# Two buffers for one tile's exponentials, a freer ScalarE order in the third tile, and a higher planner priority for four steps

## The chip, the cores and the metric

The kernel runs on one core of one Trainium2 chip. The metric is the device time of one execution in microseconds (us); of several executions the median counts. A step of the kernel is worth what it adds to the time at which the last output lands.

## The reference

The input is queries, keys and values for 4 batches, 8 heads, 576 positions and 64 dimensions a head, and the weights of two layers.

```python
scores = q @ k.T / sqrt(64)                 # heads 0-3: a local mask, 32 back; heads 4-7: a strided mask, every 32nd
attn = softmax(where(mask, scores, -1e9)) @ v
x = attn, heads side by side                # 2304 tokens x 512
h = maximum(x @ w_in1, 0)                   # first layer, 2048 wide
y = (h * h) @ w_out1
u = y @ w_in2                               # second layer
g = maximum(u, 0) + alpha * minimum(u, 0)
out = g @ w_out2
```

## The kernel before

**Tiles.** Tokens are cut into seven tiles for the first layer (`TILES`): tiles 0, 1 and 2 have 256 columns each, tiles 3 to 6 have 384. The second layer has six tiles of 384. Each tile goes through 16 slices `f` of the 2048-wide layer. One slice of one tile is a *step* `n`: steps 0 to 31 are tiles 0 and 1, interleaved by `FIRST`; steps 32 to 47 are tile 2, the third tile; then come tiles 3 to 6 and, from step 112 on, the second layer.

**One step.** Every float is carried as a high and a low part, so a product is three matmuls. `emit_h` puts 12 matmuls into the one PSUM bank `h` (line 566). `emit_g` reads that bank on ScalarE (Relu, line 578), squares it into the high part `gh` (line 579) and once more in place (line 580). `emit_gl` takes the difference on VectorE as the low part `gl` (line 594). `emit_y` adds 8 matmuls with `gh` and 4 with `gl` into the output banks (line 620). Since `h` is one bank, the matmuls of the next step's `h` wait until line 578 has read it. The second layer has lines 583 to 588 in the place of 578 to 580.

**Attention.** It is computed piece by piece while earlier tiles run. A `Unit` is local attention for some blocks: `scores` (line 245, or 249 for tiles 0 and 1), `softmax_a` on VectorE (mask and scale into the tile `e`, line 259; maximum, line 263), `softmax_b` on ScalarE (exponential with row sum, line 267), `softmax_c` (reciprocal on VectorE, lines 274 and 275; then scaling, on VectorE line 277 for tiles 0 to 2 and on ScalarE line 282 for later ones), `turn` (transposes of `e`, line 289), `turn_copy` (line 293), `values` (line 299), `emit_hi` and `emit_lo` (lines 308 and 315, the tile's `x`). `e` has one buffer, so line 259 of a unit waits for line 289 of the unit before. `Dense` is the same for the strided heads of tiles 0 and 1 (lines 340 to 400). `Strided` is strided attention of later tiles, nearly all on VectorE (lines 450, 457, 491, 498). The four units of tile 3 and its strided work are put into the iterations of the third tile (units at iterations 32, 34, 37 and 40).

**Weights.** Each of the 16 weight slots of the first layer is loaded once and converted by `convert_a` to `convert_d` on ScalarE and VectorE (lines 159 to 191), beside the steps of tiles 0 and 1. Line 191 is the last operation of a slot.

**What sets the order.** The program emits instructions in the order of `run`. SyncE issues in emission order throughout. TensorE, VectorE and GpSimd run in an order that a planner fixes when the kernel is compiled: at each point of its modelled time it gives an engine the instruction that is ready and was emitted earliest. ScalarE is under the planner up to iteration 31 and in emission order from iteration 32 on (the two `manual_schedule` regions at the end). On the chip each engine then runs its list in that order, and an instruction at its head that waits holds all behind it.

Of the kernel before, what the change touches and what calls it, by code (L numbers as in the profile page):

```python
# [16 lines left out]
P = 128  # L17
# [53 lines left out]
def attn_moe_moe2(  # L71
# [39 lines left out]
    NF = w_in1.shape[0]  # L111
# [17 lines left out]
    def psum(tag):  # L129
        return ppool.tile([P, 512], F32, tag=tag, name=f"ps_{tag}")  # L130
# [12 lines left out]
    def load_w(layer, f):  # L143

        t = wpool.tile([P, 2, 512, 2], U32, tag=f"w{f}", name="wraw")
        for h in range(2):
            src = W[layer][h][f].bitcast(U32).rearrange("p (f t) -> p f t", t=2)
            nc.sync.dma_start(out=t[:, h], in_=src)
        raws[layer, f] = t
# [48 lines left out]
    def x_tile(t):  # L198
        if t not in x_sb:
            kw = {"bufs": 1} if t == 2 else {}  # L200
            x_sb[t] = tuple(
                xpool.tile([P, NC, COLS[t]], F32R, tag=nm[:2] if t != 2 else nm, name=f"{nm}{t}", **kw)
                for nm in ("xh_c", "xl_c")
            )
        return x_sb[t]


    class Unit:


        bufs = None
# [40 lines left out]

        def softmax_a(self):
            n = self.n
            self.e = self.new("e", [P, 3, 96], bufs=1)[:, 0:n]
            self.st = apool.tile([P, 3, 4], F32, tag="st", name="stat", bufs=4)[:, :, 0:n]
            s = self.s[:, 0:96 * n].rearrange("p (n c) -> p n c", c=96)
            m = mfirst if self.first else mloc
            nc.vector.scalar_tensor_tensor(
                out=self.e, in0=s, scalar=SCALE,  # L260
                in1=m.unsqueeze(1).to_broadcast([P, n, 96]), op0=ALU.mult, op1=ALU.add,
            )
            nc.vector.tensor_reduce(out=self.st[:, 0, :], in_=self.e, op=ALU.max, axis=AX.X, negate=True)
# [284 lines left out]
    steps = [(0, t, f) for t, f in FIRST]  # L548
# [6 lines left out]
    def cols_of(n):  # L555
        return COLS[steps[n][1]] if n < SECOND else T

    def emit_h(n):
        l, t, f = steps[n]
        xh, xl = x_tile(t) if l == 0 else x2[t]  # L560
        w = wslot[l, f]
        h = psum("h")
        for c in range(NC):
            whi, wlo = w[:, 0, c * P:(c + 1) * P], w[:, 1, c * P:(c + 1) * P]
            for i, (a, b) in enumerate(((whi, xh), (whi, xl), (wlo, xh))):
                nc.tensor.matmul(  # L566
                    h[:, 0:b.shape[2]], a, b[:, c, :], start=(c == 0 and i == 0), stop=(c == NC - 1 and i == 2)
                )
        hs[n] = h

    def emit_g(n):
        l, t, f = steps[n]
        m = cols_of(n)
        h = hs.pop(n)[:, 0:m]
        g = gpool.tile([P, T], F32, tag="g", name="g")[:, 0:m]
        gh = gpool.tile([P, T], F32R, tag="gh", name="gh")[:, 0:m]
        if l == 0:
            nc.scalar.activation(out=g, in_=h, func=AF.Relu)  # L578
            nc.scalar.activation(out=gh, in_=g, func=AF.Square)  # L579
            nc.scalar.activation(out=g, in_=g, func=AF.Square)  # L580
        else:
            u = spool.tile([P, T], F32, tag="pr", name="u", bufs=2)
            nc.scalar.activation(out=g, in_=h, func=AF.Relu)  # L583
            nc.scalar.activation(out=u, in_=h, func=AF.Relu, scale=-1.0)  # L584
            nc.vector.scalar_tensor_tensor(  # L585
                out=g, in0=u, scalar=nalpha[:, f:f + 1], in1=g, op0=ALU.mult, op1=ALU.add
            )
            nc.scalar.activation(out=gh, in_=g, func=AF.Copy)  # L588
        g_sb[n] = (g, gh)

    def emit_gl(n):
        g, gh = g_sb[n]
        gl = gpool.tile([P, T], F32R, tag="gl", name="gl")[:, 0:cols_of(n)]
        nc.vector.tensor_tensor(  # L594
            out=gl, in0=g, in1=gh.bitcast(F32), op=ALU.subtract
        )
        g_sb[n] = (gh, gl)
# [70 lines left out]
    def at(when, n, fn, *args):  # L668
        when.setdefault(n, []).append((fn, args))

    def emit(when, n):
        for fn, args in when.get(n, []):
            fn(*args)
# [79 lines left out]
    def run(ns):  # L753
        for n in ns:
            l, t, f = steps[n]
            emit(starts, n)
            emit(loads, n)
            emit_gl(n)
            emit(front, n)
            if n + 1 < len(steps):  # L760
                emit_h(n + 1)
            emit(fill, n)
            emit(tensor_part, n)
            if n + 1 < len(steps):
                emit_g(n + 1)
            emit(tail_part, n)
            emit_y(n)
            if f == NF - 1:
                evac(t, l)

    outs = {}
    with tc.manual_schedule(engines={mybir.EngineType.SP}):
        def part(tag, *sizes):

            whole = wpool.tile([P, sum(sizes)], F32, tag=tag, name=f"att_{tag}")
            return [whole[:, sum(sizes[:i]):sum(sizes[:i + 1])] for i in range(len(sizes))]

        masks, de11 = part("w11", 224, 512)
        mfirst, mstr = masks[:, 0:96], masks[:, 96:224]
        bufs = {}  # L780
        for t, tags in enumerate((("w7", "w8", "w9", "w10"), ("w15", "w14", "w13", "w12"))):
            n = D * (t + 1)
            a = part(tags[0], 640, 640, 384, 384)
            v = part(tags[1], *(512,) * 4)
            pt = part(tags[2], *(512,) * 4)
            d = part(tags[3], *((512, 512, 256, 256) if t == 0 else (768, 768, 512)))
            for p in range(2):
                bufs[t, "L", p] = {
                    "qk": a[p].rearrange("p (n c) -> p n c", c=D + 96), "v": v[p][0:96].rearrange("p (n c) -> p n c", c=P),
                    "e": a[2 + p].rearrange("p (n c) -> p n c", c=96), "pt": pt[p][0:96],  # L790
                }
                bufs[t, "D", p] = {
                    "qk": d[p], "v": v[2 + p][0:n].rearrange("p (n c) -> p n c", c=P),
                    "e": d[2 + p] if t == 0 or p == 0 else de11, "pt": pt[2 + p][0:n],
                }
        units = []
        for t, kind in ORDER:
            p = sum(isinstance(x, Unit if kind == "L" else Dense) and x.t == t for x in units)
            if kind == "L":
                units.append(Unit(t, p, 0))  # L800
                units[-1].bufs = bufs[t, "L", p]
            else:
                units.append(Dense(t, p, bufs[t, "D", p]))

        def load_consts():
            nc.sync.dma_start(out=ident, in_=consts[:, 0:128])
            nc.sync.dma_start(out=mloc, in_=consts[:, 128:224])
            nc.sync.dma_start(out=masks, in_=consts[:, 224:448])

        for i, x in enumerate(units):  # L810
            x.load_qk()
            if i == 0:
                load_consts()
            if i > 0:
                units[i - 1].load_v()
            for f, w in enumerate(LOAD_AFTER):
                if w == i:
                    load_w(0, f)
        units[-1].load_v()
        for f, w in enumerate(LOAD_AFTER):  # L820
            if w >= len(units):
                load_w(0, f)
        plan()

        todo = []
        for i, unit in enumerate(units):
            for j, (name, tick) in enumerate(STAGES):
                banks = BANKS.get(name)
                args = (banks[i % len(banks)],) if banks else ()
                todo.append((i + tick + (BACK if unit.t else 0), 1, i, j, getattr(unit, name), args))  # L830
        for f, ticks in enumerate(EARLY):
            for j, (fn, tick) in enumerate(zip((convert_a, convert_b, convert_c, convert_d), ticks)):
                todo.append((tick, 0, f, j, fn, (0, f)))
        for tick, *_, fn, args in sorted(todo, key=lambda x: x[:4]):
            n = sum(tick >= x for x in TICKS)
            if n:
                at(starts, n - 1, fn, *args)
            else:
                fn(*args)
        emit_h(0)  # L840
        emit_g(0)
        run(range(2 * NF))
    with tc.manual_schedule(engines={mybir.EngineType.SP, mybir.EngineType.Activation}):
        run(range(2 * NF, len(steps)))


_OUTS = [((2304, 512), "float32")]
# [104 lines left out]
```

## Time and profile before

| | us |
|---|---|
| three runs | 894.0, 895.06, 895.51 |
| median | 895.06 |
| the profiled execution, its own time | 895.83 |
| its span in the trace | 894.0 |
| TensorE busy in the span | 870.4 |
| VectorE busy | 553.5 |
| ScalarE busy | 455.1 |

The profile's page says which engine is busy when; the windows cut the span into stretches; the waits say who waited for whom; the timelines list one engine's instructions in order, with the idle time before each and what ended it in brackets. [...] The profiled execution took 0.77 us more than the median of the runs and 1.83 us more than its span.

### The profile page before, as it was taken

The numbers are of one execution on the slowest core, as the hardware profiler recorded it, in microseconds if no ns is written. First come the engines' busy times: TensorE is split into PE (matmuls) and PEld (weight loads), VectorE is DVE, ScalarE is ACT, GpSimd is POOL, SyncE is SP. The second block draws the span as 40 slices with busy tenths as digits, with TensorE's granted clock in tenths as the row PEclk, the third lists the DMA queues.
The fourth block names the chain that finished last, engine by engine and source line by source line (L and its number), as shares of the span: only waits on it lengthen the run. The fifth ranks groups of instructions, "written<-read, shape, count | busy, mean of one in ns | idle before, by whom it ended". The sixth has DMA issues, their size and how long they took to land.

```text
span 894.0 us, 13787 instructions
## 1 busy us (share of the span) xinstructions
PE 870.4 (97%) x5448; PEld 817.4 (91%) x5448; DVE 553.5 (62%) x877; ACT 455.1 (51%) x1063; POOL 1.5 (0%) x10
## 2 busy tenths in 40 slices
PE   6799999899999999999999999999999999999997
PEld 5699989799999999999999999999999999999996
DVE  5999999949678796794598983233233333333322
ACT  6889655455545554545577664334334334334332
POOL 0000000000000000000000000000000000000000
PEclk9999999999999999999999999999999999999999
DMA  9990402111212212100687200100100100100000
GB/s 295 393 339 2 153 8 86 45 52 62 71 51 73 68 56 73 49 8 26 241 271 267 82 10 27 36 9 29 34 10 30 33 10 30 33 9 32 5 1 36
DMA packets 33537, 70.34 MB, mean 79 GB/s; under 512 B 5696, under 2 KB 17600, under 8 KB 33472
## 3 DMA queue, kind: packets, MB, share of 16 engines
q1 hardware_dynamic: 33472, 69.46, 22.8%
q8 instruction: 43, 0.70, 0.3%
q14 instruction: 22, 0.18, 0.1%
HBM read 60.01 MB, written 9.44 MB: 78 GB/s over the span
## 4 chain that ended last, share of the span: by engine, by line
PE 88%; DMA 6%; DVE 4%; ACT 1%; issue 1%; SPq 0%; ACTq 0%; DVEq 0%
PE ps_y L620 42%; PE ps_h L566 42%; DMA wraw<-in_w1o_dram 2%; DMA att_w<-in_qd_dram 1%; PE ps_o L299 1%; PE ps_s L245 1%; DMA wraw<-in_w1i_dram 1%; DMA att_w<-in_v_dram 1%; PE ps_pt L289 1%; DVE pr L491 1%; DVE ss L457 1%; DVE w L191 0%; DVE so L498 0%; DVE pr L450 0%; DVE gl L594 0%
## 5 line engine op out<-in xcount | busy, mean ns | idle before, releaser
L566 PE MATMUL ps_h<-xh_c,w 128*128 128x384 f32 (+1 forms) x896 | 221.5, 316 | 4.6 <-ACT g L578 4.2
L566 PE MATMUL ps_h<-xh,w 128*128 128x384 f32 x768 | 212.5, 337 | 0.0
L585 DVE SCALAR_TENSOR_TENSOR g<-u,nalpha,g 128x384 f32<-128x384 f32 x96 | 59.3, 618 | 193.9 <-ACT u L584 193.9
L594 DVE TENSOR_TENSOR gl<-g,gh 128x384 fp32r<-128x384 f32 (+1 forms) x208 | 108.6, 523 | 107.8 <-ACT g L580 57.9
L566 PEld LDWEIGHTS ps_h<-xh_c,w 128*128 128x128 f32 x896 | 157.9, 191 | 7.1 <-ACT g L578 5.4
L620 PE MATMUL ps_y<-gh,w 128*128 128x384 f32 (+1 forms) x896 | 158.3, 319 | 0.0
L620 PE MATMUL ps_y<-w,gh 128*128 128x512 f32 x576 | 149.0, 394 | 0.1
L566 PEld LDWEIGHTS ps_h<-xh,w 128*128 128x128 f32 x768 | 140.4, 188 | 4.2
L566 PE MATMUL ps_h<-xl_c,w 128*128 128x384 f32 (+1 forms) x448 | 140.7, 314 | 0.0
L620 PEld LDWEIGHTS ps_y<-gh,w 128*128 128x128 f32 x896 | 138.7, 190 | 1.5
L583 ACT ACTIVATE g<-ps_h 128x384 f32<-128x384 f32 x96 | 47.2, 492 | 168.5 <-PE ps_h L566 168.2
L566 PE MATMUL ps_h<-xl,w 128*128 128x384 f32 x384 | 128.9, 336 | 0.0
L578 ACT ACTIVATE g<-ps_h 128x384 f32<-128x384 f32 (+1 forms) x112 | 49.4, 441 | 151.2 <-PE ps_h L566 146.6
L620 PEld LDWEIGHTS ps_y<-w,gh 128*128 128x128 f32 x576 | 106.6, 188 | 17.2 <-ACT gh L588 0.6
L620 PE MATMUL ps_y<-gl,w 128*128 128x384 f32 (+1 forms) x448 | 86.2, 313 | 2.0 <-DVE gl L594 1.9
L566 PEld LDWEIGHTS ps_h<-xl_c,w 128*128 128x128 f32 x448 | 85.5, 191 | 0.1
L588 ACT ACTIVATE gh<-g 128x384 fp32r<-128x384 f32 x96 | 50.5, 526 | 68.1 <-DVE g L585 68.1
L620 PE MATMUL ps_y<-w,gl 128*128 128x512 f32 x288 | 82.0, 392 | 0.0
L566 PEld LDWEIGHTS ps_h<-xl,w 128*128 128x128 f32 x384 | 72.1, 188 | 4.1
L620 PEld LDWEIGHTS ps_y<-gl,w 128*128 128x128 f32 x448 | 71.7, 189 | 2.6 <-DVE gl L594 2.6
L620 PEld LDWEIGHTS ps_y<-w,gl 128*128 128x128 f32 x288 | 54.1, 188 | 12.5
L579 ACT ACTIVATE gh<-g 128x384 fp32r<-128x384 f32 (+1 forms) x112 | 53.8, 480 | 2.9
(98 smaller groups left out, 840.7 us busy)
## 6 DMA issues: line engine op xcount, KB each, us to landing
wraw<-in_w1i_dram SPq DMA_DIRECT2D x16, 512.0 KB, 8.8
wraw<-in_w1o_dram SPq DMA_DIRECT2D x16, 512.0 KB, 9.1
wraw<-in_w2i_dram SPq DMA_DIRECT2D x16, 512.0 KB, 3.7
wraw<-in_w2o_dram SPq DMA_DIRECT2D x16, 512.0 KB, 4.7
qk<-in_qk_dram SPq DMA_DIRECT2D x16, 336.0 KB, 3.8
out_dram<-ev SPq DMA_DIRECT2D x18, 256.0 KB, 2.3
y<-ev SPq DMA_DIRECT2D x16, 192.0 KB, 2.0
x2raw<-y SPq DMA_DIRECT2D x16, 192.0 KB, 3.2
```

The lines of the kernel that those rows point to most:

```text
L245: nc.tensor.matmul(s, self.qk[:, j, 0:P], self.qk[:, j, P:], start=True, stop=True)
L289: nc.tensor.transpose(self.pt_ps[0:96, P * j:P * j + P], self.e[:, j, :], ident)
L299: nc.tensor.matmul(self.o[64 * h:64 * h + 64, 64 * j:64 * j + 64], self.v[:, j, D * h:D * h + D], self.pt[:, P * j + 64 * h:P * j + 64 * h ...
L457: nc.vector.tensor_reduce(out=self.s[:, b, r:r + ROWS, j0:j1], in_=pr, op=ALU.add, axis=AX.X)
L566: nc.tensor.matmul(h[:, 0:b.shape[2]], a, b[:, c, :], start=(c == 0 and i == 0), stop=(c == NC - 1 and i == 2))
L578: nc.scalar.activation(out=g, in_=h, func=AF.Relu)
L579: nc.scalar.activation(out=gh, in_=g, func=AF.Square)
L583: nc.scalar.activation(out=g, in_=h, func=AF.Relu)
L585: nc.vector.scalar_tensor_tensor(out=g, in0=u, scalar=nalpha[:, f:f + 1], in1=g, op0=ALU.mult, op1=ALU.add)
L588: nc.scalar.activation(out=gh, in_=g, func=AF.Copy)
L594: nc.vector.tensor_tensor(out=gl, in0=g, in1=gh.bitcast(F32), op=ALU.subtract)
L620: nc.tensor.matmul(y, a, b, start=(f == 0 and i == 0 and (l, t) != (0, 1)), stop=(f == NF - 1 and i == 2), skip_group_check=(l == 0 and t ...
```

## The change

The tile `e` of `Unit.softmax_a` gets two buffers. `emit_gl` and `emit_g` are emitted at high priority in every step: the planner treats them as if they stood at the program's start. The same holds for the steps of tile 0's attention that are emitted ahead of step 0, and for `emit_h(0)` and `emit_g(0)`. The region in which ScalarE is under the planner reaches over the third tile, to iteration 47. No operation is added or removed.

```diff
         def softmax_a(self):
             n = self.n
-            self.e = self.new("e", [P, 3, 96], bufs=1)[:, 0:n]
+            self.e = self.new("e", [P, 3, 96], bufs=2)[:, 0:n]
...
             emit(loads, n)
-            emit_gl(n)
+            with tc.high_priority():
+                emit_gl(n)
             emit(front, n)
...
             if n + 1 < len(steps):
-                emit_g(n + 1)
+                with tc.high_priority():
+                    emit_g(n + 1)
             emit(tail_part, n)
...
                 at(starts, n - 1, fn, *args)
+            elif getattr(getattr(fn, "__self__", None), "t", 1) == 0:
+                with tc.high_priority():
+                    fn(*args)
             else:
                 fn(*args)
-        emit_h(0)
-        emit_g(0)
-        run(range(2 * NF))
+        with tc.high_priority():
+            emit_h(0)
+            emit_g(0)
+        run(range(3 * NF))
     with tc.manual_schedule(engines={mybir.EngineType.SP, mybir.EngineType.Activation}):
-        run(range(2 * NF, len(steps)))
+        run(range(3 * NF, len(steps)))
```

## Rows read from the trace of the kernel before

**Rows 1.** Windows: stretch, length, busy (count) of PE, PEld, DVE, ACT, POOL, then clock, DMA.

```profile
20.00:180.00 160.00, 149.05 (x1331) 141.79 (x1326) 153.40 (x262) 111.03 (x276) 0.83 (x3) 0.98 0.42 148
180.00:200.00 20.00, 20.00 (x177) 19.60 (x176) 7.85 (x17) 11.20 (x33) 0.00 (x0) 1.00 0.18 58
200.00:850.00 650.00, 650.00 (x3616) 611.88 (x3615) 370.00 (x553) 307.70 (x680) 0.28 (x1) 1.00 0.18 60
```

**Rows 2.** Windows of 5 us in which TensorE idles.

```profile
30.00:35.00 5.00, 3.45 (x36) 2.92 (x34) 4.90 (x12) 5.00 (x19) 0.00 (x0) 1.00 1.02 409
40.00:45.00 5.00, 3.12 (x30) 2.70 (x31) 4.64 (x10) 5.00 (x10) 0.00 (x0) 0.85 1.03 401
...
125.00:130.00 5.00, 3.34 (x28) 3.14 (x27) 5.00 (x10) 1.60 (x4) 0.00 (x0) 1.00 0.00 0
...
160.00:165.00 5.00, 2.29 (x11) 2.29 (x12) 5.00 (x9) 2.38 (x7) 0.00 (x0) 0.79 0.00 0
```

**Rows 3.** Waits of TensorE: total us, times, longest.

```profile
PE ps_h L566 <- ACT g L578: 4.2, 1, 4.2
...
PE ps_y L620 <- DVE gl L594: 1.9, 2, 1.7
```

**Rows 4.** Timeline of ScalarE: start, us, instruction, idle before it and its releaser.

```profile
123.04 0.42 ACT L580 ACTIVATE g<-g 128x256 f32<-128x256 f32 x1
...
158.60 0.37 ACT L267 ACTIVATE e<-e,stat 128x96 f32<-128x96 f32 x1 [4.06 <-DVE stat L263]
...
161.48 0.90 ACT L282 ACTIVATE e<-e,stat 128x96 f32<-128x96 f32 x3 [1.70 <-DVE stat L275]
162.29 0.36 ACT L578 ACTIVATE g<-ps_h 128x256 f32<-128x256 f32 x1
```

**Rows 5.** Timeline of VectorE in the same stretch of the third tile.

```profile
156.97 0.45 DVE L259 SCALAR_TENSOR_TENSOR e<-ps_s,mloc 128x288 f32<-128x288 f32 x1
...
158.07 0.44 DVE L263 TENSOR_REDUCE stat<-e 128x3 f32<-128x288 f32 x1
...
161.22 0.17 DVE L275 RECIPROCAL stat<-stat 128x3 f32<-128x3 f32 x1
```

**Rows 6.** Chain that ended last: start, us, merged instructions, behind the stall and later.

```profile
162.71 2.77 PE ps_h L566 x12
165.47 0.84 PE ps_o L299 x12
...
171.16 1.44 PE ps_h L566 x12
172.60 0.50 PE ps_o L299 x12
...
198.16 2.08 PE ps_h L566 x12
```

**Rows 7.** Timeline of VectorE from 124 to 137 us.

```profile
124.14 1.67 DVE L457 TENSOR_REDUCE ss<-pr 128x10 f32<-128x640 f32 x2
...
126.86 0.42 DVE L594 TENSOR_TENSOR gl<-g,gh 128x256 fp32r<-128x256 f32 x1
...
136.58 0.28 DVE L315 TENSOR_TENSOR xl_c<-ps_o,xh_c 128x128 fp32r<-128x128 f32 x1
```

**Rows 8.** Timeline of VectorE in the first 62 us.

```profile
14.74 0.69 DVE L351 SCALAR_TENSOR_TENSOR att_w<-ps_s,att_w 128x512 f32<-128x512 f32 x1 [1.15 <-PE ps_s L340]
...
24.98 0.69 DVE L400 TENSOR_TENSOR xl_c<-ps_y,xh_c 128x512 fp32r<-128x512 f32 x1 [1.09 <-ACT xh_c L394]
...
61.69 1.22 DVE L191 TENSOR_TENSOR w<-wt,w 128x1024 fp32r<-128x1024 f32 x1
```

**Rows 9.** Timeline of TensorE: `h` of step 9, a wait for `gl`, `h` of step 32.

```profile
63.50 0.38 PE L566 MATMUL ps_h<-xh_c,w 128*128 128x256 f32 x1
...
127.33 0.74 PE L620 MATMUL ps_y<-gl,w 128*128 128x256 f32 x4 [1.66 <-DVE gl L594]
...
139.41 0.40 PE L566 MATMUL ps_h<-xh_c,w 128*128 128x256 f32 x2
```

## Prediction

> **What bounds the kernel now.** I read the windows first, to see where TensorE idles, because it is busy nearly everywhere. From 200 to 850 us it has no idle time [rows 1]: 650 us of 650. Whatever the new priorities do there, they can't shorten it; they can only do harm. All that can be had lies ahead of 180 us: in the stretch from 20 to 180 us TensorE lacks 160 - 149.05 = 10.95 us [rows 1]. In the same stretch VectorE is busy 153.40 us of 160 and ScalarE 111.03. So in that stretch VectorE is as full as TensorE, and it feeds TensorE through `gl`, through the weights and through the attention. Second I read the windows of 5 us, to see where the idle time lies: about 1.5 to 1.9 us each at 30 to 35 and 40 to 45, then 1.66 at 125 to 130, then the largest piece at 160 to 165 [rows 2]. Third the waits of TensorE name what ended them: one wait of 4.2 us for line 578 (`g`), and two for line 594 (`gl`) with 1.9 us together, the longer 1.7 [rows 3]. Fourth the timelines of ScalarE and VectorE show why `g` and `gl` were late.
>
> **Part 1: the stall in the third tile** (two buffers, ScalarE unordered, `g` at high priority). Line 578 at 162.29 stands behind line 267 and line 282 of a tile-3 unit in the order written out for ScalarE. Line 267 made ScalarE idle for 4.06 us and line 282 for another 1.70 [rows 4]. What they waited for is VectorE: line 259 of that unit starts at 156.97 and line 263 at 158.07, between strided operations, and line 275 comes at 161.22, again behind strided work [rows 5]. While ScalarE waited, the `h` bank was full and not read, so TensorE idled 4.2 us [rows 3], to 162.71 [rows 6]. [...] The 12 `h` matmuls after the stall took 2.77 us where the same 12 later took 1.44, and the 12 of line 299 took 0.84 where they later took 0.50 [rows 6]. The price of the stall is 4.2 + 1.33 + 0.34 = 5.87 us.
>
> Each of the three edits works on this stall. With two buffers line 259 need not wait for the transposes of the unit before. With ScalarE under the planner and `g` first among what is ready, line 578 goes as soon as the bank is full, some 6 us earlier here, and the softmax lines fill the gaps. I take the whole 5.87 us. The lower bound is 0 (the planner's list puts lines 267 and 282 ahead of line 578 all the same); the upper bound is the 5.87. Cover that remains: ScalarE has room (111.03 us of 160, rows 1), so running `g` first delays nothing that is due; tile 3's `x` is due at 198.16 us, where the `h` matmuls of its first step begin (2.08 us for twelve, not 1.44) [rows 6], and VectorE has 12.15 us of 20 free from 180 to 200 [rows 1].
>
> [...] The idle time at 125 to 130 us, 1.66 us, left the granted clock at 1.00 [rows 2], so a stall that shrinks to that size would give back the 1.67 us of slow matmuls too.
>
> **Part 2: `gl` at high priority.** `g` of that step was ready when line 580 ended at 123.46 [rows 4], and `gl` ran at 126.86 [rows 7]: VectorE first did strided work that was emitted earlier (the line 457 pair at 124.14 among it). TensorE waited 1.66 us for it, to 127.33 [rows 9]. At high priority `gl` waits for the operation under way alone, at most about 0.8 us here (half of the pair's 1.67), and ends by about 124.7, ahead of 127.33 - 1.66 = 125.67, when TensorE ran dry. I take 1.66 us, and 0.2 for the shorter wait for `gl` [rows 3]. Bounds 0 and 1.9. What moves back on VectorE is 0.42 us of strided or weight work for each `gl` put ahead.
>
> **Part 3: the start** (tile 0's attention, `h(0)`, `g` and `gl` of the first steps at high priority). VectorE idles 1.15 us before line 351, an operation of tile 1 that stands at the head of its list while its scores aren't there, and 1.09 us before line 400 of tile 0, at the end of that tile's chain [rows 8]. With tile 0 first both pieces may be filled: 2.24 us. Against it, one `g` group (0.36 + 0.42 + 0.42 = 1.2 us, rows 4) now goes ahead of tile 1's exponentials on a ScalarE that is full from 30 to 45 us [rows 2], and tile 1's `x` is what steps 4 and 5 wait for. Bounds: a loss of 1.2 us and a gain of 3.4 us, the idle time of TensorE in the first two windows of rows 2. I take half of the 2.24, 1.1 us, since only one of the two tiles is put first.
>
> **Part 4: everything behind.** High priority for VectorE's share of `g` and `gl` in the other steps, and the second buffer for tiles 4 to 6, move operations beside a TensorE that never waits [rows 1]: nothing. The cover is VectorE's spare time there, 650 us less its busy time in rows 1; without it each `gl` of 0.42 us [rows 7] would push other work back by as much.
>
> **The sum.** 5.87 + 1.66 + 0.2 + 1.1 = 8.83 us. The profiled execution took 895.83, which makes 887.0 of it; that run is 0.77 above the median, so the median becomes 895.06 - 8.83 = 886.2 us. VectorE's due times allow it, though narrowly: the weights of step 9 are ready at 62.91 and used at 63.50 [rows 8, 9], a margin of 0.6 us, and the last low part of tile 2's `x` is ready at 136.86 and used at 139.41 [rows 7, 9], 2.55 us. Parts 2 and 3 bring TensorE forward by 2.96 us at that point, but part 3 comes from VectorE's own idle time, so VectorE is 1.1 us earlier too, and 1.86 us fit into 2.55.
>
> **The rivals.**
> *VectorE gives the gain back.* Up to 180 us VectorE's work is fixed, and if it is what TensorE follows, an earlier `g` only moves the wait to the weights or to `x`. Then only VectorE's idle time can be won, 160 - 153.40 = 6.6 us at the most, and half of it by the share that I took in part 3: 895.06 - 3.3 = 891.8 us. For it: 96% busy and a margin of 0.6 us. Against it: from 180 to 200 us VectorE works only 7.85 us of 20 [rows 1], so it had finished tile 3's work long before it was due, and the largest stall was no lack of VectorE time but the order on ScalarE. [...]
>
> *The planner's list holds `g` up more often.* Slower. The planner orders ScalarE by modelled times; if VectorE's strided operations take longer on the chip than it assumes, lines 267 and 282 of each of the four tile-3 units stand at ScalarE's head before their inputs exist, with `g` behind them. The price is that of the stall now, 5.87 us a unit. One unit is blocked so far; with two the sum is 895.06 - 2.96 + 5.87 = 898.0, with three 903.8. It decides from one and a half units on. For it: VectorE is full and its operations last 1 us and more, so modelled ready times drift. Against it: iterations up to 31 already run under the planner beside an equally full VectorE, and from 50 to 155 us TensorE waited there for 1.9 us only, for `gl` [rows 3].
>
> *The change does nothing here.* The planner puts about the same order, or another operation of VectorE is as late: 895.
>
> **How the numbers follow.** The forecast has 0.60 and the own range 884 to 889 (part 3 between its bounds). VectorE giving back has 0.16, at 889 to 893. No effect has 0.08. More blocked units have 0.16, from 897 to 904. The range 882.5 to 897 leaves out most of the last case and little below. A difference of 0.2%, 1.8 us, is about what a measurement can tell from no change. Faster by more than that: 0.60 + 0.16 = 0.76; within: 0.08; slower: 0.16.
>
> **What would show it.** Right: no wait of TensorE for line 578 and none over 0.5 us for line 594; a granted clock of 1.00 from 125 to 200 us; on ScalarE line 578 directly after the last `h` matmul in iterations 32 to 47; tile 3's first `h` matmuls about 9 us earlier than 198.16. Wrong by the first rival: new waits for line 191 or line 315. Wrong by the second: idle time on ScalarE before lines 267 or 282 with line 578 behind. Part 3 is seen in the time at which step 4 begins. Any new TensorE idle time between 200 and 850 us would break part 4.

## The result and the profile after

The changed kernel takes 905.12 us (median of 9 runs, 903.94 to 905.82), the kernel before 895.51 in the same session: a ratio of 1.0092, 95% interval 1.0069 to 1.0114. By the medians it is slower by 9.6 us, with 886.2 us forecast and a range that ended at 897. The profiled execution of after has a span of 904.0 us, 10.0 more than before. Executions of one and the same kernel can fall into groups 4 (`one_block`) to 11 us (`warm_again`) apart.

The waits of TensorE in the trace of after (columns as in [rows 3]) no longer show lines 578 and 594, the two that the forecast was about:

```profile
PE ps_y L620 <- ACT gh L579: 3.0, 3, 1.1
PE ps_pt L289 <- issue: 2.9, 1, 2.9
...
PE ps_pt L289 <- DVE stat L275: 2.0, 1, 2.0
```

The windows of after answer to [rows 1]. From 20 to 180 us TensorE is now busier (154.22 us, 149.05 before), and behind 200 us it is full as before. It isn't idle time that made the kernel slower there.

```profile
20.00:180.00 160.00, 154.22 (x1294) 142.95 (x1293) 138.87 (x243) 108.99 (x271) 0.56 (x2) 0.98 0.42 146
180.00:200.00 20.00, 20.00 (x183) 19.60 (x182) 19.03 (x30) 11.35 (x36) 0.28 (x1) 1.00 0.32 99
200.00:850.00 650.00, 650.00 (x3651) 612.49 (x3650) 372.57 (x557) 308.57 (x685) 0.28 (x1) 1.00 0.18 59
```

A milestone in both traces tells where the time went: line 578, ScalarE's reading of `h`, runs once a step. Its timeline in after, at steps 0, 4 and 37 (start, duration, instruction, idle time before):

```profile
41.24 0.38 ACT L578 ACTIVATE g<-ps_h 128x256 f32<-128x256 f32 x1 [2.83 <-PE ps_h L566]
...
71.80 0.36 ACT L578 ACTIVATE g<-ps_h 128x256 f32<-128x256 f32 x1
...
172.76 0.39 ACT L578 ACTIVATE g<-ps_h 128x256 f32<-128x256 f32 x1 [1.56 <-PE ps_h L566]
```

The same line in before, at steps 0 and 4 (step 37 is in [rows 4], at 162.29):

```profile
27.80 0.38 ACT L578 ACTIVATE g<-ps_h 128x256 f32<-128x256 f32 x1 [0.68 <-PE ps_h L566]
...
50.73 0.39 ACT L578 ACTIVATE g<-ps_h 128x256 f32<-128x256 f32 x1
```

After is 13.44 us late at step 0 and 21.07 at step 4, and never lost more. At step 37 it is 10.47 late, and from step 48 on about 10.1 up to the end. So the start lost 21.07 us, and everything behind it won 11.0. Step by step the gains are these: 2.31 us between steps 27 and 28 (the stall for `gl` of [rows 9]), 6.22 between steps 36 and 37 (the stall of [rows 4]), and 2.4 in small pieces.

How the 21 us came about is seen from two windows, from the start to step 4, first in before, then in after:

```profile
0.00:50.73 50.73, 38.54 (x450) 32.15 (x451) 38.46 (x82) 36.32 (x109) 0.37 (x6) 0.97 0.99 349
```

```profile
0.00:71.80 71.80, 54.62 (x458) 43.09 (x459) 41.70 (x85) 39.12 (x112) 0.38 (x6) 0.95 0.75 261
```

Nearly the same matmuls (450 and 458) took 16.1 us more of TensorE's time; idle time grew by only 21.07 - 16.08 = 5.0 us. So a matmul at the start became slower, by 39% on average (54.62 / 458 against 38.54 / 450). The timeline of TensorE shows two reasons, first in after, then in before:

```profile
18.01 1.06 PE L289 MATMUL ps_pt<-ident,att_w 128*96 128x128 f32 x4 [2.91 <-issue]
19.76 0.48 PE L299 MATMUL ps_o<-att_w,att_w 96*64 96x64 f32 x2 [0.68 <-ACT att_w L293]
20.16 0.66 PE L289 MATMUL ps_pt<-ident,att_w 128*96 128x128 f32 x2
20.76 0.48 PE L299 MATMUL ps_o<-att_w,att_w 96*64 96x64 f32 x2
...
29.43 0.42 PE L372 MATMUL ps_pt<-ident,att_w 128*64 128x128 f32 x1
29.78 0.42 PE L385 MATMUL ps_y<-att_w,att_w 64*32 64x64 f32 x2
...
47.33 1.47 PE L385 MATMUL ps_o<-att_w,att_w 128*32 128x64 f32 x32
...
53.64 1.11 PE L385 MATMUL ps_o<-att_w,att_w 128*32 128x64 f32 x32
```

```profile
14.62 1.12 PE L299 MATMUL ps_o<-att_w,att_w 96*64 96x64 f32 x16
15.68 0.85 PE L289 MATMUL ps_pt<-ident,att_w 128*96 128x128 f32 x4
17.60 0.69 PE L299 MATMUL ps_y<-att_w,att_w 96*64 96x64 f32 x16 [1.07 <-ACT att_w L293]
```

**Turns.** Calls are taken in turn: one matmul of line 299 (two entries in the view), one or two of line 289, again one of line 299, and later 372 and 385. In before each call was a row of its own (16 entries of line 299, then 4 of line 289). High priority puts each block at the start of the program, and here each of the 36 calls of tile 0's attention (four units, nine calls each) is a block of its own; so the first instructions of all blocks stand level, then the second ones. ScalarE shows the same: it takes two exponentials of line 267, then goes on to other units, and comes to the last ones only at 14.80 and 15.16. So VectorE's line 274 starts at 15.82, and not at 10.66 as in before, and the first line 289 at 18.01, not at 11.73:

```profile
8.05 0.36 ACT L267 ACTIVATE att_w<-att_w,stat 128x96 f32<-128x96 f32 x1
...
10.27 0.37 ACT L267 ACTIVATE att_w<-att_w,stat 128x96 f32<-128x96 f32 x1 [1.77 <-DVE stat L263]
...
15.16 0.36 ACT L267 ACTIVATE att_w<-att_w,stat 128x96 f32<-128x96 f32 x1
```

**Pace.** In before the fast pace comes at some 16 us: 16 entries of line 299 took 1.12 us at 14.62 and 0.69 at 17.60. In after line 385 still needs 1.47 us for 32 entries at 47.33 and 1.11 for the same at 53.64, and as far as like entries can be compared, every matmul up to about 48 us runs at about half pace (line 566 comes every 0.21 us at 46.56 and every 0.12 at 55.50). The column of the granted clock, a share of full speed, says 1.00 at the start of both traces (from 0 to 40 us in before, from 0 to 60 in after). The experiments show that it can't be trusted there.

### The profile page after: what moved, and what is told of

It is laid out like the page before. It is cut to its first block, busy times and chain, and to the rows that moved or that the text cites. A ratio compares the mean times of both kernels' runs of the same rounds, so it can differ in the third digit from the quotient of the medians.

```text
span 904.0 us, 13783 instructions
## 1 busy us (share of the span) xinstructions
PE 881.7 (98%) x5448; PEld 825.3 (91%) x5448; DVE 553.7 (61%) x877; ACT 454.7 (50%) x1063; POOL 1.5 (0%) x10
## 4 chain that ended last, share of the span: by engine, by line
PE 96%; ACT 2%; DMA 1%; SPq 0%; issue 0%; DVE 0%; ACTq 0%
PE ps_h L566 45%; PE ps_y L620 45%; PE ps_o L299 2%; PE ps_s L245 1%; PE ps_pt L289 1%; DMA att_w<-in_qd_dram 1%; PE ps_y L385 1%; PE ps_pt L372 0%; PE ps_y L340 0%; ACT wraw L159 0%; ACT att_w L267 0%; PE ps_o L385 0%; PE ps_s L249 0%; PE ps_y L299 0%; ACT att_w L356 0%
## 5 line engine op out<-in xcount | busy, mean ns | idle before, releaser
L620 PEld LDWEIGHTS ps_y<-w,gh 128*128 128x128 f32 x576 | 106.6, 188 | 17.3 <-ACT gh L588 0.6
L580 ACT ACTIVATE g<-g 128x384 f32<-128x384 f32 (+1 forms) x112 | 53.8, 480 | 2.9
```

Source lines behind the costliest of these rows:

```text
L620: nc.tensor.matmul(y, a, b, start=(f == 0 and i == 0 and (l, t) != (0, 1)), stop=(f == NF - 1 and i == 2), skip_group_check=(l == 0 and t ...
```

## The experiments

Medians are in us; of the kernel before they are 895.5 to 896.9 by session. Each ratio is to the kernel before in the same session, with its 95% interval, and is not simply the ratio of the medians.

### Which part lost the time

`no_start`: the changed kernel without its edits of the start.

```diff
-            elif getattr(getattr(fn, "__self__", None), "t", 1) == 0:
-                with tc.high_priority():
-                    fn(*args)
...
-        with tc.high_priority():
-            emit_h(0)
-            emit_g(0)
+        emit_h(0)
+        emit_g(0)
```

> The changed kernel without its edits at the start: tile 0's attention, h(0) and g(0) have their ordinary priority again; the two buffers, g and gl first, and ScalarE under the planner in the third tile stay. If the loss lies in the start alone and the gains behind it are their own (2.4 us at step 28 and 6.2 us at step 37 in the changed kernel's trace, 8 to 9 in all): 886 to 888 us. If those gains only came because the late start gave VectorE time to catch up: 893 to 896.

Measured: 889.02, ratio 0.9924 (0.9899 to 0.9949). Step 4 is 3.02 us late, step 48 is 6.71 early.

`start_only`: the kernel before with these edits alone.

```diff
+            elif getattr(getattr(fn, "__self__", None), "t", 1) == 0:
+                with tc.high_priority():
+                    fn(*args)
...
+        with tc.high_priority():
+            emit_h(0)
+            emit_g(0)
```

> The kernel before with the edits at the start alone. If they cost the 19 to 21 us by which steps 4 to 27 are late in the changed kernel's trace, and the two later stalls are still there: 912 to 916 us; if the late start lets VectorE catch up so that one or both stalls vanish: 905 to 910. If the start were harmless and g or gl first did the harm: 895.

Measured: 912.9, ratio 1.0191 (1.0176 to 1.0206). Both old stalls are still in its waits, the same `issue` wait is new:

```profile
PE ps_h L566 <- ACT g L578: 4.9, 4, 4.0
...
PE ps_pt L289 <- issue: 2.9, 1, 2.9
PE ps_y L620 <- DVE gl L594: 2.6, 2, 2.3
```

By the medians (896.56 for the kernel before, measured beside both) the start alone loses 16.3 us and the rest alone wins 7.5. The difference, 8.8, is the 9.6 of the result but for 0.8, no more than the 1 us by which the median of the kernel before moved from one set of runs to the other.

### Which of the start's edits, and how

`no_att`: the changed kernel, tile 0's attention in ordinary order, `emit_h(0)` and `emit_g(0)` still first.

```diff
-            elif getattr(getattr(fn, "__self__", None), "t", 1) == 0:
-                with tc.high_priority():
-                    fn(*args)
```

> The changed kernel with tile 0's attention at ordinary priority, but h(0) and g(0) still first. If the attention's blocks make the loss: 885 to 889 us. If h(0), whose matmuls are taken between the others as soon as their inputs are there, makes it: 900 to 906.

Measured: 886.41 (four executions at 886.03 to 887.29, the profiled one at 892.98), ratio 0.9911 (0.9882 to 0.9939). So the attention's blocks carry the loss, 905.1 - 886.4 = 18.7 us. The one trace of `no_att` is of the 892.98 execution; none of the four faster ones was traced.

`one_block`: the attention of tile 0 stays first, but as one block in place of 36.

```diff
+        todo = sorted(todo, key=lambda x: x[:4])
+        first = []
+        with tc.high_priority():
+            for tick, *_, fn, args in todo:
+                if tick < TICKS[0] and getattr(getattr(fn, "__self__", None), "t", 1) == 0:
+                    first.append(fn)
+                    fn(*args)
+        for tick, *_, fn, args in todo:
...
-            elif getattr(getattr(fn, "__self__", None), "t", 1) == 0:
-                with tc.high_priority():
-                    fn(*args)
+            elif fn in first:
+                pass
```

(`emit_h(0)` and `emit_g(0)` are in ordinary order here.)

> The changed kernel with tile 0's attention at high priority as one block, emitted in one go, and h(0) and g(0) at ordinary priority. In the changed kernel each of the 36 calls is a block of its own that begins at the program's start, so that the planner takes the first instruction of every call before the second of any. If this taking of turns is what costs: the start is at least as early as in the kernel before, 884 to 889 us. If it costs to put tile 0 ahead of the weights and of tile 1 at all: 900 to 906.

Measured: 891.75 (two groups, 888.79 to 889.90 and 893.61 to 894.66), ratio 0.9932 (0.9901 to 0.9962). The turns are gone from its trace, and most of the loss with them. It is the 36 separate blocks that harm: the faster group is as fast as `no_start` (889.02), which also has `emit_h(0)` and `emit_g(0)` in ordinary order. That being first costs nothing at all isn't shown, since half of the executions are in the second group, and the median lies 2.75 us above the expected range because of it.

`att_pe` and `att_act`: the changed kernel with blocks for TensorE's calls alone, and for those of ScalarE and VectorE alone.

```diff
-            elif getattr(getattr(fn, "__self__", None), "t", 1) == 0:
+            elif getattr(getattr(fn, "__self__", None), "t", 1) == 0 and fn.__name__ in ("scores", "turn", "values"):
...
-            elif getattr(getattr(fn, "__self__", None), "t", 1) == 0:
+            elif getattr(getattr(fn, "__self__", None), "t", 1) == 0 and fn.__name__ not in ("scores", "turn", "values"):
```

> The changed kernel, but of the first tile's attention only the calls that run on TensorE (scores, turn, values) stand in high-priority blocks of their own; the calls of ScalarE and VectorE have the ordinary order. Theory (the loss is TensorE taking turns between calls, one matmul of each shape after another): most of the loss stays, 899 to 906 us, with lines 289 and 299 alternating on TensorE. Rival (the loss is ScalarE and VectorE taking turns between units, so that the first unit is finished late): the loss goes, 886 to 893 us.

> The changed kernel, but of the first tile's attention only the calls that run on ScalarE and VectorE stand in high-priority blocks of their own; scores, turn and values have the ordinary order, so TensorE runs each call as one row of equal matmuls. Theory (the loss is TensorE taking turns): 886 to 893 us. Rival (the loss is ScalarE and VectorE taking turns between units): 899 to 906 us. If both this and the run beside it lose about half, 893 to 899 us, both kinds of turns count.

Measured: 898.58 (ratio 1.0019, 1.0001 to 1.0038) and 897.98 (0.9996, 0.9965 to 1.0026). Each of the two kinds alone loses about 12 us against `no_att`, both together 18.7. Neither theory had that alone; the third case that was named (both count) fits. Why the two don't add up can be argued from the traces. In that of `att_pe` the matmuls were fast at 15.43 us and, 9 us later, slow while they took turns, and this time the windows' clock column has it, 0.82 and then 0.50 (the window from 15 to 20 us also holds 1.5 us of idle time):

```profile
15.00:20.00 5.00, 3.49 (x30) 2.05 (x24) 4.01 (x11) 2.88 (x11) 0.00 (x0) 0.82 1.03 396
20.00:25.00 5.00, 5.00 (x34) 3.18 (x33) 2.71 (x7) 2.08 (x9) 0.00 (x0) 0.50 1.05 296
25.00:30.00 5.00, 5.00 (x66) 3.58 (x65) 1.65 (x3) 2.02 (x4) 0.00 (x0) 0.50 1.02 408
```

The timeline of TensorE in `att_pe`:

```profile
15.43 0.32 PE L289 MATMUL ps_pt<-ident,att_w 128*96 128x128 f32 x1
...
24.30 0.42 PE L372 MATMUL ps_pt<-ident,att_w 128*64 128x128 f32 x1
```

This single row of line 372 takes 0.42 us at a granted clock of 0.50. The same row in after, at 29.43, takes 0.42 under a clock column of 1.00. So by its durations after was at half clock there too, and its column says 1.00 from 0 to 60 us, over matmuls of either pace.

In `att_act`, where TensorE runs each call in a row, ScalarE's turns left it idle before the first line 289 (2.9 us, as in after), and its 32 entries of line 385 at 33.35 still took 1.92 us, where the same in before took 1.11 at 19.69; it was slow to beyond 35 us. So in both traces TensorE is slow for 10 us and more at a time when before is fast, and a pace that is slow already can't be lost a second time. How the turns would bring the slow pace, by an idle wait or by broken rows, isn't shown: the traced execution of `no_att`, without these turns, was slow up to 35 us too (32 entries of line 385 took 1.93 us at 29.36). What differs is how often an execution is long: one of five of `no_att`, eight of ten of `att_act` (the other two took 893.7), while all ten of `att_pe` lie within 2.4 us and all nine of after within 1.9.

### The slow pace by itself

`warm`: the changed kernel with 33 early matmuls that nothing reads.

```diff
+        blank = cpool.tile([P, P], F32, name="blank")
+        nc.vector.memset(blank, 0.0)
+        idle = psum("y2")
+        for k, lhs in ((12, blank), (5, units[0].bufs["qk"][:, 0, 0:P]), (4, units[1].bufs["qk"][:, 0, 0:P])):
+            for _ in range(k):
+                nc.tensor.matmul(idle[:, 0:P], lhs, blank, start=True, stop=True)
...
                 with tc.high_priority():
                     fn(*args)
+                if fn == units[0].softmax_b:
+                    idle = psum("y3")
+                    for _ in range(12):
+                        nc.tensor.matmul(
+                            idle[0:4, 0:P], units[0].st[:, 1, :], blank, start=True, stop=True
+                        )
```

> The changed kernel with 33 matmuls more, which nothing reads: 12 of 128 x 128 at the very start, 9 more that wait for the first and the second unit's queries and keys, and 12 with four columns of weights and 128 columns of data that wait for the first unit's row sums and fill TensorE's idle time ahead of the first line 289. High-priority blocks stay as they are, and so do the turns on ScalarE and VectorE and nearly all turns on TensorE. [...] Rival (the loss is the turns alone; the pace hardly matters, since TensorE waits for other engines): 902 to 908 us, also if the fast pace comes early. If the fast pace doesn't come early, the run tells nothing on this.

Measured: 890.89 (four executions at 890.30 to 891.07, the profiled one at 898.91), ratio 0.9941 (0.9922 to 0.9960). More work on TensorE, the turns of lines 299, 289, 372 and 385 still there, and 14.2 us less time than after. If the slow pace was a part of the loss of its own, 893 to 899 us were expected; the result lies 2 us below that range. `warm_again` is the same kernel once more:

> The changed kernel with 33 early matmuls, once more, for a trace of an execution in which the pace stays high. Theory: 890 to 892 us; the trace shows lines 372 and 385 alternating at some 0.2 to 0.26 us a switch, not 0.35, up to line 578 of step 4, some 5 us ahead of the 63.50 us of the other execution. Rival: a trace like the other one and still about 891 us, so that the fall of the pace was not what made that execution longer.

Measured: 890.78 (seven executions at 890.25 to 892.21, one at 901.48), ratio 0.9935 (0.9894 to 0.9976); the profiled execution is one of 890.8. The two traces of one program make the cleanest pair of the study. In the windows of `warm`, the 898.91 execution, the clock falls between 20 and 25 us:

```profile
20.00:25.00 5.00, 5.00 (x34) 3.01 (x35) 3.01 (x7) 1.01 (x5) 0.00 (x0) 0.62 1.04 313
25.00:30.00 5.00, 5.00 (x33) 2.99 (x33) 2.06 (x4) 2.33 (x5) 0.00 (x0) 0.50 1.03 402
```

In those of `warm_again` it doesn't, and 89 matmuls go through in the 5 us that held 33 (not all of the same lines, since `warm_again` is further on by then):

```profile
20.00:25.00 5.00, 5.00 (x53) 3.17 (x49) 3.54 (x9) 2.61 (x6) 0.00 (x0) 1.00 1.04 318
25.00:30.00 5.00, 5.00 (x89) 4.17 (x88) 2.82 (x7) 2.29 (x4) 0.00 (x0) 1.00 1.03 395
```

One turn of line 372 takes 0.30 us at full clock, the first row here from `warm_again`, and 0.42 at half, the second from `warm`:

```profile
23.66 0.30 PE L372 MATMUL ps_pt<-ident,att_w 128*64 128x128 f32 x1
```

```profile
27.11 0.42 PE L372 MATMUL ps_pt<-ident,att_w 128*64 128x128 f32 x1
```

Step 4 comes 9.3 us later in `warm` than in `warm_again`, and the end 8.1 us later. Of the 9.3 us, 1.1 were lost before the clock fell (ten entries of line 299 start at 20.82 and at 19.71). The other 8.2 are the price of about 20 us at half clock (21 to 42 us). In after the slow pace lasts to about 48 us, 32 us longer than in before; at the same rate that would be 13 us. `warm` took 14.2 off, of which 1.2 are not pace, since the added matmuls also moved the first line 289 from 18.01 to 16.77. By both ways some 13 of the 18.7 us are pace. This is an estimate: `warm` came to the fast pace within the first 8 us, which before didn't.

`warm_no_att` and `warm_no_start` were to give the price of the turns alone: early matmuls, attention in ordinary order, the second one without the priority of `emit_h(0)` and `emit_g(0)`, too.

```diff
+        def keep_busy(k, lhs):
+            for _ in range(k):
+                nc.tensor.matmul(idle[:, 0:P], lhs, blank, start=True, stop=True)
+
+        keep_busy(12, blank)
...
-            elif getattr(getattr(fn, "__self__", None), "t", 1) == 0:
-                with tc.high_priority():
-                    fn(*args)
             else:
                 fn(*args)
+                for i, k in ((0, 11), (1, 4)):
+                    if fn == units[i].scores:
+                        keep_busy(k, units[i].bufs["qk"][:, 0, 0:P])
```

> The changed kernel with the first tile's attention in ordinary order, and 27 early matmuls that nothing reads (12 at the start, 11 behind the first unit's scores, 4 behind the second's). Theory (the pace carried most of the loss, the turns the rest): as fast as the same kernel without the added matmuls when that one went over to the fast pace early, 885 to 887.5 us, and no executions near 893 us; against 890.9 us with the turns, these cost 4 to 5 us. Rival (with the fast pace the turns cost nothing, and the early matmuls only add work): 889 to 892 us.

> As the run beside it, but with the first `h` and `g` in ordinary order too. Expected from the two kernels without the added matmuls, 889.0 and 886.4 us: 887 to 889.5 us. If early matmuls change the planner's order more than the pace, the two come out the other way round.

Measured: 892.93 (889.94 to 895.71; ratio 0.9947, 0.9922 to 0.9972) and 892.03 (889.23 to 895.53; 0.9945, 0.9918 to 0.9972). Both missed. All 12 matmuls stand ahead of the first unit's scores here, only six of them do in `warm`, so line 249 starts at 6.46 us and not at 3.91; and the clock fell in spite of them, to 0.54 from 30 to 35 us in `warm_no_att`. Nothing follows for the turns. Between `warm_again` and `no_att` lie 890.8 - 886.4 = 4.4 us, and at step 4 `warm_again` is 3.48 us behind the kernel before, `no_start` without any turns 3.02. But `warm_again` also has an earlier fast pace: the second 16 entries of line 249 take 0.88 us there (at 7.73) and 1.54 in `no_start`, and none of the four shorter executions of `no_att` was traced. So neither difference bounds the price of the turns.

### What a turn costs on TensorE

`probe`: the changed kernel with 384 matmuls behind its last output, in rows of 32: one shape alone, then two in turn.

```diff
+        last = psum("y0")
+        def square(c0=0):
+            nc.tensor.transpose(last[0:128, c0:c0 + 128], ident, ident)
+        def narrow():
+            nc.tensor.matmul(last[0:64, 128:192], ident[0:96, 0:64], ident[0:96, 0:64], start=True, stop=True)
...
+        for fns in ((square,), (square,), (narrow,), (square, narrow), (square,), (rows,), (square, rows),
+                    (cols,), (square, cols), (quarter,), (square, quarter), (cols, quarter)):
+            for _ in range(32 // len(fns)):
+                for fn in fns:
+                    fn()
```

> The changed kernel with 384 matmuls appended behind its last output, into a bank that is free by then; nothing reads them. They come in rows of 32: one shape alone, then two shapes in turn: square (128 rows of weights by 128 columns, the shape of a transpose), narrow (96 by 64, the shape of line 299), rows (96 by 128), cols (128 by 64), quarter (128 by 32, the shape of line 385). [...] Rival (shapes in turn cost no more than the mean of the two rows): at most 0.05 us more than that mean, and the slow pace at the start has another cause.

The timeline of TensorE in `probe` (line 854 is square, 857 narrow, 860 is 96 x 128; a matmul of these counts as two entries, a transpose as one):

```profile
900.29 7.21 PE L854 MATMUL ps_y<-ident 128*128 128x128 f32 x64 [0.24 <-ACT ev L641]
907.42 3.94 PE L857 MATMUL ps_y<-ident 96*64 96x64 f32 x64
...
911.56 0.33 PE L857 MATMUL ps_y<-ident 96*64 96x64 f32 x2
911.82 0.33 PE L854 MATMUL ps_y<-ident 128*128 128x128 f32 x1
912.08 0.33 PE L857 MATMUL ps_y<-ident 96*64 96x64 f32 x2
...
917.28 0.48 PE L857 MATMUL ps_y<-ident 96*64 96x64 f32 x2
917.69 0.48 PE L854 MATMUL ps_y<-ident 128*128 128x128 f32 x1
...
927.36 8.76 PE L860 MATMUL ps_y<-ident 96*128 96x64 f32 x64
```

In a row a square takes 7.21 / 64 = 0.11 us and a narrow one 3.94 / 32 = 0.12. In turn each takes 0.26 (912.08 - 911.82) at full clock: this change of shape costs 0.14 us, more than the rival's 0.05. At half clock each takes 0.41 (917.69 - 917.28), the figure of after's start. A price of turns had been expected as 0.35 to 0.4 us a matmul, which is close to the half-clock figure only. The windows of `probe` show the clock before and behind the fall at about 915.8 us, and then around a second one:

```profile
911.30:913.30 2.00, 2.00 (x14) 1.31 (x12) 0.00 (x0) 0.00 (x0) 0.00 (x0) 1.00 0.00 0
...
917.60:921.70 4.10, 4.10 (x17) 2.36 (x15) 0.00 (x0) 0.00 (x0) 0.00 (x0) 0.50 0.00 0
...
927.40:932.80 5.40, 5.40 (x52) 5.40 (x50) 0.00 (x0) 0.00 (x0) 0.00 (x0) 1.00 0.01 3
932.90:935.90 3.00, 3.00 (x16) 3.00 (x16) 0.00 (x0) 0.00 (x0) 0.00 (x0) 0.50 0.00 0
```

The first time the clock fell while TensorE was counted busy all the time and did nothing but take turns. The second time it fell in the middle of the unbroken row of line 860, with no turns at all. And square and 128 x 64 in turn, at 0.26 us a matmul as well, stayed at 1.00 throughout (949.3 to 957.5 us). So turns are neither needed for a fall nor enough for one, and what brought the two falls stays open.

### The gains taken one by one

`prio_only`, `act_only`, `e2_only`: the kernel before with the priority of `g` and `gl` alone, with ScalarE under the planner alone, with the two buffers alone.

```diff
+            with tc.high_priority():
+                emit_gl(n)
...
+                with tc.high_priority():
+                    emit_g(n + 1)
```

```diff
-        run(range(2 * NF))
+        run(range(3 * NF))
...
-        run(range(2 * NF, len(steps)))
+        run(range(3 * NF, len(steps)))
```

```diff
-            self.e = self.new("e", [P, 3, 96], bufs=1)[:, 0:n]
+            self.e = self.new("e", [P, 3, 96], bufs=2)[:, 0:n]
```

> The kernel before with one edit alone: the `g` and `gl` of every step at high priority; one buffer for `e`, ScalarE in emission order in the third tile, the start as it was. Theory (the stalls are separate): the wait for line 594 near 125 us (1.66 us) goes, and the stall of the third tile stays whole (a wait for line 578 of about 4 us), because ScalarE runs there in emission order; 895 - 2 = 892 to 894.5 us. Rival (priority is the main part of the gain of the later stages): the stall of the third tile goes too, 886 to 889 us.

> The kernel before with one edit alone: ScalarE under the planner up to the end of the third tile; one buffer for `e`, ordinary priority. Theory (the stall of the third tile was the order written out for ScalarE): no wait for line 578 near 160 us, step 48 some 5 to 6 us earlier, the wait for line 594 near 125 us still there; 889 to 890.5 us. Rival (the planner puts lines 267 and 282 ahead of line 578 as well, since they were emitted earlier): the wait stays, or comes more often, 894 to 900 us.

> The kernel before with one edit alone: two buffers for `e`. Theory (the second buffer doesn't touch what ScalarE waited for, VectorE's lines 259 and 263 between strided operations, and only moves line 259 a little): the stall of the third tile stays between half and whole, 892 to 895.5 us. Rival (line 259 was late because the buffer was not free): the stall goes by this edit alone, 889 to 890 us.

Measured: 891.44 (0.9947, 0.9923 to 0.9971), 890.52 (0.9945, 0.9918 to 0.9971), 890.3 (0.9938, 0.9905 to 0.9971). Each of the three alone removes the third tile's stall (`prio_only` leaves a wait of 0.9 us of the 4.2); two of three expectations were wrong on that. They do it in different ways. With two buffers VectorE takes line 259 before the strided work, at 151.28 and not 156.97 [rows 5], and ScalarE's line 267 finds its input ready. VectorE, then ScalarE of `e2_only`:

```profile
151.28 0.45 DVE L259 SCALAR_TENSOR_TENSOR e<-ps_s,mloc 128x288 f32<-128x288 f32 x1
```

```profile
155.04 0.36 ACT L267 ACTIVATE e<-e,stat 128x96 f32<-128x96 f32 x1
```

With the priority the planner's order on VectorE moves, and line 259 comes at 152.87. With ScalarE free, line 267 is no earlier than before, and line 578 passes it (ScalarE of `act_only`):

```profile
157.12 0.39 ACT L578 ACTIVATE g<-ps_h 128x256 f32<-128x256 f32 x1 [1.90 <-PE ps_h L566]
...
160.86 0.38 ACT L267 ACTIVATE e<-e,stat 128x96 f32<-128x96 f32 x1 [2.18 <-DVE stat L263]
```

So the single gains are 5.1, 6.0 and 6.2 us, 17.3 in sum, and 7.5 together in `no_start`, which also holds the gain at the stall for `gl`: one stall, taken away three times.

`gl_e2_act`: the kernel before with two buffers, ScalarE free and `gl` alone at high priority.

```diff
-            emit_gl(n)
+            with tc.high_priority():
+                emit_gl(n)
```

(and the second and third of the diffs above)

> The kernel before with three edits: two buffers for `e`, ScalarE under the planner to the end of the third tile, and `gl` alone at high priority (`g` and the start as they were). Theory (the stall of the third tile is worth 5 to 6 us, taken once whichever edit removes it, the one for `gl` 2 us, and the 2.5 us that the kernel with the two priorities alone lost at step 2 come from `g`): 895.5 - 5.8 - 2 = 887 to 888.5 us. Rival (the loss at step 2 comes from `gl`, or VectorE gives it back): 889.5 to 891 us.

Measured: 889.35, ratio 0.9908 (0.9875 to 0.9942), between the two expectations. It is 2.98 us late at step 2, where `prio_only` was 2.49 late, so the priority of `gl` brings that early loss, not only `g`. The gain at the stall for `gl` (2.3 us) about pays for it: at step 28 it stands at +0.26.

## Why the prediction was wrong

**The step that failed is part 3, the start.** It had a gain of 1.1 us, with a lower bound of -1.2. In truth the start lost 21 us by step 4, 18 of them more than `no_start`. Two things were missing in that step.

First, it costed the edit as "tile 0 goes ahead of tile 1", from VectorE's idle time in [rows 8]. But the edit wraps each call by itself, and each block restarts at the program's start. That was to be read in the code: 36 blocks that stand level. The instructions *within* tile 0 change their order, and `one_block` shows that this was the harm. The rival that ended slower had its mechanism in the third tile, and 36 turns at the start stood in no rival.

Second, it took TensorE's matmul durations at the start as given. The part asked what ScalarE and VectorE do and never what the pace depends on. Some 13 of the 18.7 us, by the estimate above, are matmuls at the slow pace, where before had gone over to the fast one at some 16 us; `warm`, with 33 early matmuls, won 14.2 us. Part 1 of the prediction had priced slow matmuls behind a stall (1.67 us, at a granted clock of 0.79 over 160 to 165 us [rows 2]), and the same question was not asked of the start of the program. The trace's clock column would not have helped, since it says 1.00 there; the durations show the pace.

On turns, the probe measured 0.14 us a change between 128 and 64 columns at full clock. Between 128 and 96 rows a change showed no price (0.53 us a pair in turn, from 936.45 to 936.98, at a granted clock of 0.50, where twice the times in a row at 1.00, 0.21 and 0.11, make 0.64). The prediction had no term for turns.

**Part 1 was right in size:** 5.87 us forecast, 6.22 between steps 36 and 37. Its reading, ScalarE's order held up by VectorE, held; that all three edits are needed was never claimed, and each one does it alone.

**Part 2 was right:** 1.86 forecast, 2.31 between steps 27 and 28, no wait for line 594 left. What it left out is an early price: with `gl` ahead, step 2 comes 2.5 to 3 us later.

**Part 4 held:** no idle time of TensorE from 200 to 850 us, and a granted clock of 1.00 from 125 to 850 us.

Parts 1, 2 and 4 together were 7.73 us; `no_start`, which is the change without part 3, won 7.5. That the two are so close is in part luck: `no_start` lost 3.02 us by step 4, which no part had, and made it up by gains somewhat above those forecast and by small ones that no part names. Of the 18.9 us between forecast and result some 17.2 are part 3's: the 1.1 that didn't come and the 16.1 between `no_start` and after. Most of the other 1.7 is the median of the kernel before, 896.56 in the session of `no_start` and 895.06 in the forecast.

**The rivals.** *VectorE gives the gain back* would have left 3.3 us, or 891.8; `no_start` at 889.02 won more than twice that, and no wait for line 191 or line 315 is new in after. The early loss at step 2 isn't of its kind by the waits: the new one of `no_start` is for ScalarE (1.4 us for line 579). *The planner's list holds `g` up* would have shown waits for line 578 in the third tile; there are none in after. The result came out on that rival's side, 1.1 us above its range of 897 to 904, with a cause that wasn't its.

**What stays open:** what sets the time at which the clock rises: some 16 us in the trace of before, some 35 in that of the 892.98 execution of `no_att`. Up to 16 us TensorE runs the same entries at the same pace in both, but with more idle time in `no_att` (2.79 us in place of 1.81 before its second line 249); whether that decides isn't shown. With it stays open how the 36 blocks keep the pace low, of which only the frequency is shown. The price of the turns alone is open too: 4.4 us by `warm_again`, but the two executions of `att_act` at 893.7, which have ScalarE's and VectorE's turns alone, lie 7.3 above `no_att`, and neither of them was traced.

**A version that beats both kernels** is `no_att` at 886.41 (five executions, one of them at 892.98), the change without the attention's blocks.

## What to carry to other kernels

A priority that restarts for each call does not put a group first, it makes its members take turns; one block around the group keeps their order. At the start of a program ask of any reordering whether TensorE still comes to its fast pace as early as before (some 16 us before, about 48 us after in this case), and read the pace from the duration of one recurring instruction (line 372: 0.42 us in after under a column of 1.00, as in `att_pe` at 0.50) rather than from the clock column. When several edits of a change work on one stall, price the stall once.

## What the runs showed of the hardware that was not expected

In `probe` a change between matmuls of 128 and 64 weight columns cost 0.14 us at full clock, more than either matmul (0.11 and 0.12 us). TensorE's granted clock fell from 1.00 to 0.50 twice while it was counted busy all the time, once while it took turns (at about 915.8 us) and once in an unbroken row of one shape (at about 932.8 us). And 33 matmuls whose results nothing reads, placed in the first 18 us, made a kernel of 905 us faster by 14.2 us.
